# Attention of two pairs of heads as one task on TensorE, with the gates loaded first, more g buffers and a float32 combine

## Chip, cores and metric

The kernel runs on one core of a Trainium2 chip. The metric is the device time of one execution in microseconds. TensorE is called PE in the profile, VectorE DVE, ScalarE ACT, GpSimd POOL; SyncE (SP) issues every DMA of this kernel.

## What is computed

Three layers follow each other, on 4 batches of 576 positions (2304 tokens), 8 heads of 64:

```
scores = q k^T / 8, causal; plus min(-(cum_i - cum_j), 0), cum = cumsum(max(s, 0))
attn   = softmax(scores);  x = attn v            -> 2304 x 512
h      = x w_in;  g = max(h, 0)^2;  x = g w_out  (512 -> 2048 -> 512; int64 views of float64 weights come in)
logits = x phi                                   (32 slots = 8 experts x 4)
slot_input = softmax over tokens(logits)^T x     -> 32 x 512
slot_out[e] = max(slot_input[e] w1[e], 0) w2[e]  (512 -> 1024 -> 512, 8 experts)
out    = softmax over slots(logits) slot_out     -> 2304 x 512
```

## The kernel before

One program does all of it. Every step is a task in a list (`add`) with the buffers that it reads and writes, a cost for each engine that may run it, and a priority. At build time `Plan.run` walks through the list with a clock of its own and writes the engines' instruction order: it takes the task that can start first, among those within `WAIT` the one of lowest priority number, and on TensorE it prefers a task with the tiling that TensorE already has, unless another is `SAME` (6) steps ahead. A task can be placed only when its buffers are free. On the chip each engine runs its list in that order.

The tasks, in the order of the data:

- **Attention.** 80 steps: 4 batches, 5 blocks `i` of 128 queries (the fifth has 64), 4 pairs of heads `p`. `a_scores` (L654 to L700) computes both heads of a pair into two PSUM banks of the pool `ps_s` (four banks); the two heads lie on the two halves of TensorE's rows (tiling 64x128). The maxima are taken on VectorE (L682, L696), `a_exp` (L705) on ScalarE frees the banks, `a_norm` scales, splits into float16 high and low parts (L446) and sends them through a DMA transpose (L746). `a_pv` (L768 to L822) multiplies with V (tiling 128x64, L805) `LAG` (2) steps after the scores. Batch 0 stays in float32 and is transposed on TensorE (L758, through the pool `ps_h`, two banks). Four pairs fill one tile of x.
- **The hidden layer**, for 18 tiles of 128 tokens and 4 column blocks each: `m_h` (L838, 12 matmuls at L847 in two tasks, into a bank of `ps_h`), then relu and square into a buffer `g` (L862 to L866), `m_t` (transposes, L887), `m_l` (logits, L904), and for each two tiles `m_s` (L927: running softmax over tokens, and L966, which reads the eight g buffers of both tiles and frees them). The first evacuation waits for `h_scale` (L828), which needs the scales of all four column blocks of w_in.
- **Weights.** 16 blocks of w_in and 16 of w_out^T are loaded, `N_RAW` (6) ahead, and converted from float64 bits on ACT, POOL and DVE in the first 105 us. When the attention's probability buffers (`p_p`) are done with, their space goes to w_out (16 loads) and to w1 and w2 of the experts (64 pieces of 512 KB, 33.5 MB): more than the space, so later pieces wait until PE has used up something.
- **Experts and combine.** `hidden` (L1277) and `project` (L1295) for each expert; `m_c` (L978) makes the softmax over slots in bfloat16 parts, and `combine` (L1302) multiplies: the slot outputs are split into two bfloat16 parts by DVE (L1312 to L1315), 36 pairs of matmuls (L1326, L1327) write 18 banks, ACT and DVE copy them out, SP sends 12 DMAs.

A partition has 207 KB. By the sizes in the code the pools that are opened at the start take 192,672 bytes; of the 19,296 left `gt` takes five buffers (10,240) and `x` three (6,144), and of what remains one buffer of g (2,048 bytes) fits; the other g buffers come when the pools of the conversion are done with.

Of the kernel before, what the change touches and what calls it, by code (L numbers as in the profile page):

```python
# [7 lines left out]
F32 = mybir.dt.float32  # L8
# [14 lines left out]
N_QK = 2  # L23
D_COST = 1.08
# [9 lines left out]
N_RAW = 6  # L34
SBUF = 207 * 1024
GB1 = 4
GB2 = 8
# [9 lines left out]
N_OB = 5  # L47
# [13 lines left out]
N_W32 = 7  # L61
LAG = 2
# [16 lines left out]
CT_LATE = 0  # L79
# [273 lines left out]
def attention_moe_softmoe(ctx, tc, qk, v, s, w_in, w_out, w_out_t, phi, w1, w2, cst, out):  # L353
# [27 lines left out]
    def fixed(shape, dt):  # L381
# [43 lines left out]
        "vhl": (vhl_p, 5, [128, 2, 512], F16), "ph": (ph_p, 2, [128, 2048], F16), "x2": (x_p, X2, [128, 2, KD, 128], F16), "v": (v_p, 0, [128, 512], F32),  # L425
# [228 lines left out]
    def a_scores(P, i):  # L654


        sel = biases[P]
        if plain(P):
            r, sc, col = raws[P], cs, lambda k: -0.125
            qk = [r]  # L660
            terms = [(lambda d, c: r.t[d, 0, c], lambda d, c: r.t[d, 1, c])]
        else:
            sc, col = scal[P]
            qk = qs, ks = stacks[P]
            terms = [(lambda d, c, e=e: qs.t[d, e, c], lambda d, c, f=f: ks.t[d, f, c]) for e, f in HALVES]
        n = 128 * (i + 1)
        m, nm = small["m"].new(), small["nm"].new()
        pss = [ps_s.new(), ps_s.new()]
        D = [slice(64 * h, 64 * h + 64) for h in range(2)]
        if i < 4:  # L670
            def mul():
                for j, (q_, k_) in enumerate(terms):
                    for h, ps in enumerate(pss):
                        nc.tensor.matmul(ps.t[:, 0:n], q_(D[h], slice(128 * i, 128 * i + 128)), k_(D[h], slice(0, n)), start=j == 0, stop=False)  # L674
                for k in range(2):
                    for h, ps in enumerate(pss):
                        nc.tensor.matmul(ps.t[:, n - 128 + 64 * k:n], rows_h.t[D[h], k, :], mask.t[D[h], k, 64 * k:128], start=False, stop=False)
                for h, ps in enumerate(pss):
                    nc.tensor.matmul(ps.t[:, 0:n], sel.t[D[h], :], cum3.t[D[h], 0:n], start=False, stop=True)  # L679
            add([*qk, sel, mask, cum3, rows_h], pss, P=((5 if plain(P) else 4) * (5 + n / 2.4) + 80, mul), tiling=(64, 128))  # L680
            for h, ps in enumerate(pss):
                add([ps], [(m, 2 + h)], V=(60 + 1.04 * n, lambda ps=ps, h=h: nc.vector.reduce_max(out=m.t[:, 2 + h:3 + h], in_=ps.t[:, 0:n], axis=AX.X)))  # L682
        else:
            for ps, c0, c1 in ((pss[0], 0, 512), (pss[1], 512, 576)):
                def mul(ps=ps, c0=c0, c1=c1):
                    o = [ps.t[d, 0:c1 - c0] for d in D]
                    for j, (q_, k_) in enumerate(terms):
                        for h, d in enumerate(D):
                            nc.tensor.matmul(o[h], q_(d, slice(512, 576)), k_(d, slice(c0, c1)), start=j == 0, stop=False)  # L689
                    if c0:  # L690
                        for h, d in enumerate(D):
                            nc.tensor.matmul(o[h], rows_h.t[d, 0, 0:64], mask.t[d, 0, 0:64], start=False, stop=False)
                    for h, d in enumerate(D):
                        nc.tensor.matmul(o[h], sel.t[d, 0:64], cum3.t[d, c0:c1], start=False, stop=True)
                add([*qk, sel, mask, cum3, rows_h], [ps], P=(880 if c0 == 0 else 180, mul), tiling=(64, 64))
                add([ps], [(m, c0 // 512)], V=(60 + 1.04 * (c1 - c0), lambda ps=ps, c0=c0, c1=c1: nc.vector.reduce_max(out=m.t[:, c0 // 512:c0 // 512 + 1], in_=ps.t[:, 0:c1 - c0], axis=AX.X)))  # L696
            add([(m, 0), (m, 1)], [(m, 2)], V=(65, lambda: nc.vector.tensor_tensor(out=m.t[:, 2:3], in0=m.t[:, 0:1], in1=m.t[:, 1:2], op=ALU.max)))
# [70 lines left out]
    def a_pv(P, i):  # L768
        b, p = P
        if p == 0:  # L770
            xps[b, i] = ps_x0.new()
        x = xps[b, i]
        c0 = 128 * p
        c1 = c0 + (128 if i < 4 else 64)
        mms = []
        if whole(P[0], i):
            vv, pt = [vraw[b, j] for j in range(i + 1)], a_transpose(P, i)
            f = lambda: pt.t.bitcast(F32)
            for j in range(i + 1):
                def two(h, j=j):  # L780
                    k_ = slice(0, 64 if j == 4 else 128)
                    o = 128 * (h * (i + 1) + j) if i < 4 else 128 * j + 64 * h
                    return vv[j].t[k_, 128 * p + 64 * h:128 * p + 64 * h + 64], f()[k_, o:o + c1 - c0]
                mms.append(two)
            ns = 268 * len(mms) - 30 if i < 4 else 170 * len(mms)
        else:
            vv, pt = [vhl[b, j] for j in range(i + 1)], pts.pop((P, i))
            V = lambda e, j, h, k=128: vv[j].t[0:k, e, 128 * p + 64 * h:128 * p + 64 * h + 64]
            T = lambda: pt.t.rearrange("p (j q) -> p j q", q=128)
            for j in range(min(i + 1, 4)):  # L790
                for e, f in ((0, 0), (0, 1), (1, 0)):
                    if i < 4:
                        mms.append(lambda h, j=j, e=e, f=f: (V(e, j, h), T()[:, (2 * h + f) * (i + 1) + j, :]))
                    else:
                        mms.append(lambda h, j=j, e=e, f=f: (V(e, j, h), T()[:, j + 5 * f, 64 * h:64 * h + 64]))
            if i == 4:
                mms.append(lambda h: (V(0, 4, h), T()[:, 4, 64 * h:64 * h + 64]))
                mms.append(lambda h: (V(1, 4, h, 64), T()[0:64, 4, 64 * h:64 * h + 64]))
            ns = (57 if i < 4 else 38) * len(mms) + 10
# [178 lines left out]
    def m_c(t0, n):  # L978

        c1, c4, pc, w = small["c1"].new(), c4_p.new(), ps_t.new("c"), n * NS  # L980
# [4 lines left out]
        part = lambda j: c4.t[:, 0:n, j, :]  # L985
# [8 lines left out]
        for j in range(3):  # L994
            add(L_, [(c4, j)], V=(130 + 0.52 * w, lambda j=j: nc.vector.tensor_copy(out=part(j), in_=c())),
                A=(93 + 0.834 * w, lambda j=j: nc.scalar.copy(out=part(j), in_=c())))
            if j == 0:
                add([(c4, 0)], [(c4, 3)], G=(161 + 0.834 * w, lambda: nc.gpsimd.tensor_copy(out=part(3), in_=part(0))))
            if j < 2:
                add([(c4, j)], L_, V=(60 + 1.04 * w, lambda j=j: nc.vector.tensor_tensor(out=c(), in0=c(), in1=part(j), op=ALU.subtract)))  # L1000
        ph = lambda: pc.t.bitcast(BF16)

        def turn():
            for k in range(n):
                nc.tensor.transpose(ph()[:, k * 128:(k + 1) * 128], c4.t[:, k].rearrange("p a n -> p (a n)"), ident_h.t)
        add([c4, ident_h], [pc], P=(60 * n, turn))
        evacuate(lambda: ct.t[:, t0:t0 + n, :], lambda: ph()[:, 0:n * 128].rearrange("p (t q) -> p t q", q=128), n * 128, [pc], [(ct, t0)], "VA")
# [91 lines left out]
    def prepare(x):  # L1099
# [295 lines left out]
```

## Time and profile before

| | us |
|---|---|
| median of the runs (568.04, 568.16; a third, at 1643.59, stands apart) | 568.16 |
| profiled execution, its time | 565.6 |
| its span, first to last instruction | 563.8 |
| busy in the span: PE / DVE / ACT / POOL | 494.1 / 375.0 / 321.8 / 222.6 |
| moved by DMA | 102.70 MB, mean 182 GB/s |

The profiled execution is one run with the profiler on. "Busy" is the time in which at least one instruction of the engine was in flight; matmuls are pipelined, so a busy PE may still have room. A line number is a line of the kernel before.

### The profile page before, as it was taken

To read this page: it belongs to the slowest core of one execution; us is meant where nothing else is said; L and a number is where in the kernel's file an instruction comes from. 1 tells how busy PE (TensorE), PEld (TensorE's weight loads), DVE (VectorE), ACT (ScalarE), POOL (GpSimd) and SP (SyncE) were. 2 spreads that over 40 slices of the span, in tenths; PEclk is the share of its full clock that TensorE was granted. 3 is DMA by queue.
4 is the path that set the end of the run, shared out by engine and by line. 5 is a ranking of instruction groups with operands and counts; after the bars stand their busy time and mean duration, and the time that the engine had idled before them with its cause. 6 is when DMAs were issued, how large, how long until landed. Compare 5 with 4: busy or idle time off the path is not lost. (4 is left out here: it accounts for less than half of the span.)

```text
span 563.8 us, 13264 instructions
## 1 busy us (share of the span) xinstructions
PE 494.1 (88%) x5025; PEld 277.9 (49%) x5025; DVE 375.0 (67%) x948; ACT 321.8 (57%) x802; POOL 222.6 (39%) x351
## 2 busy tenths in 40 slices
PE   0377688989999999999999999999999989889873
PEld 0244344656555555655546565555554544434333
DVE  2888988979989777899976648986456451210022
ACT  2768777768766675676654555664555545310023
POOL 3478786756425433565662313524132210000000
PEclk9999778999999999999999999999999999989998
DMA  8988566144646753566643113465098999699938
GB/s 254 348 281 293 197 222 195 38 141 128 146 85 123 121 121 71 123 148 136 141 87 74 31 29 57 94 113 94 6 228 306 287 330 382 249 331 409 409 121 335
DMA packets 107464, 102.70 MB, mean 182 GB/s; under 512 B 80904, under 2 KB 81032, under 8 KB 107400
## 3 DMA queue, kind: packets, MB, share of 16 engines
q1 hardware_dynamic: 107400, 101.86, 61.9%
q8 instruction: 39, 0.64, 0.4%
q14 instruction: 25, 0.20, 0.1%
HBM read 77.85 MB, written 4.72 MB: 146 GB/s over the span
## 5 line engine op out<-in xcount | busy, mean ns | idle before, releaser
L847 PE MATMUL bank<-sbuf 128*128 128x512 f16 x864 | 201.7, 379 | 1.3 <-ACT sbuf L820 0.8
L847 PEld LDWEIGHTS <-sbuf 128*128 128x128 f16 x864 | 81.8, 98 | 88.8 <-issue 4.1
L440 POOL TENSOR_SCALAR sbuf<-sbuf 128x512 f16<-128x512 f32 (+9 forms) x128 | 95.6, 753 | 63.4 <-DVE sbuf L728 16.7
L705 ACT ACTIVATE sbuf<-bank,sbuf 128x512 f32<-128x512 f32 (+4 forms) x160 | 93.4, 589 | 40.6 <-DVE sbuf L699 30.6
L457 ACT COPY sbuf<-bank 128x512 f32<-128x512 f32 (+6 forms) x129 | 59.5, 475 | 98.1 <-PE bank L887 31.6
L446 DVE SCALAR_TENSOR_TENSOR sbuf<-sbuf 128x512 f16<-128x512 f32 (+5 forms) x146 | 105.3, 748 | 9.9 <-POOL sbuf L440 9.1
L682 DVE TENSOR_REDUCE sbuf<-bank 128x1 f32<-128x128 f32 (+3 forms) x128 | 57.6, 480 | 5.2 <-PE bank L679 4.9
L674 PE MATMUL bank<-sbuf 64*128 64x128 f16 (+7 forms) x352 | 47.0, 363 | 15.0 <-DMA sbuf<-in_qk_dram 14.1
L727 POOL TENSOR_SCALAR sbuf<-sbuf 128x2 f32<-128x2 f32 (+1 forms) x66 | 18.1, 274 | 106.4 <-ACT sbuf L705 71.5
L862 ACT ACTIVATE sbuf<-bank,sbuf 128x512 f32<-128x512 f32 x56 | 38.4, 686 | 35.2 <-PE bank L847 35.1
L513 POOL TENSOR_SCALAR sbuf<-sbuf 128x512 int32<-128x512 uint8 x47 | 35.6, 757 | 56.5 <-DMA sbuf<-in_w_out_dram 27.5
L805 PE MATMUL bank<-sbuf 128*64 128x128 f16 (+4 forms) x1296 | 55.1, 228 | 1.5 <-DVE sbuf L446 0.7
L458 DVE COPY sbuf<-bank 128x512 f32<-128x512 f32 (+7 forms) x63 | 32.0, 512 | 31.8 <-PE bank L887 18.3
L887 PE MATMUL bank<-sbuf 128*128 128x128 f32 x288 | 45.4, 280 | 5.1 <-POOL sbuf L864 2.0
L463 ACT ACTIVATE sbuf<-sbuf 128x512 bf16<-128x512 f32 (+1 forms) x60 | 39.0, 651 | 13.2 <-DVE sbuf L515 11.5
L515 DVE SCALAR_TENSOR_TENSOR sbuf<-sbuf 128x512 int32<-128x512 int32 x48 | 35.6, 747 | 14.7 <-POOL sbuf L513 11.7
L887 PEld LDWEIGHTS bank<-sbuf 128*128 128x128 f32 x288 | 33.2, 142 | 20.4 <-ACT sbuf L865 3.7
L510 ACT ACTIVATE sbuf<-sbuf 128x512 f32<-128x512 f32 x48 | 31.6, 671 | 16.1 <-DMA sbuf<-in_w_out_dram 7.7
L805 PEld LDWEIGHTS <-sbuf 128*64 128x64 f16 (+1 forms) x1056 | 28.8, 110 | 17.4 <-issue 16.4
L758 PE MATMUL bank<-sbuf 128*128 128x128 f32 (+1 forms) x100 | 19.6, 314 | 14.3 <-POOL sbuf L440 13.1
L705 ACT ACTIVATION_READ_ACCUMULATOR sbuf<-bank,sbuf 128x1 f32 x160 | 32.0, 200 | 0.0
L865 ACT ACTIVATE sbuf<-sbuf 128x512 f32<-128x512 f32 x44 | 27.7, 630 | 4.8 <-DVE sbuf L863 3.7
(140 smaller groups left out, 664.2 us busy)
## 6 DMA issues: line engine op xcount, KB each, us to landing
sbuf<-in_w_dram SPq DMA_DIRECT2D x48, 512.0 KB, 10.1
sbuf<-in_qk_dram SPq DMA_DIRECT2D x16, 576.0 KB, 6.2
sbuf<-in_w_in_dram SPq DMA_DIRECT2D x16, 512.0 KB, 10.1
sbuf<-in_w_out_t_dram SPq DMA_DIRECT2D x16, 512.0 KB, 5.2
sbuf<-in_w_out_dram SPq DMA_DIRECT2D x16, 512.0 KB, 4.4
sbuf<-in_w_dram SPq DMA_DIRECT2D x32, 256.0 KB, 5.4
sbuf<-in_v_dram SPq DMA_DIRECT2D x28, 256.0 KB, 3.0
out_dram<-sbuf SPq DMA_DIRECT2D x8, 512.0 KB, 4.5
```

Source lines behind the costliest of these rows:

```text
L440: "G": (244 + 0.834 * n, lambda: nc.gpsimd.tensor_scalar(out=out_(), in0=in_(), scalar1=scale(), scalar2=1.0, op0=ALU.mult, op1=ALU.mult)),
L446: alts = {"V": (base + 1.04 * n, lambda: nc.vector.scalar_tensor_tensor(out=out_(), in0=in_(), scalar=scale(), in1=hi(), op0=ALU.mult, op1 ...
L457: "A": (51 + 0.834 * n, lambda: nc.scalar.copy(out=out_(), in_=in_())),
L463: add(r + [junk], w, A=(186 + 0.834 * n, lambda: nc.scalar.activation(out=junk.t[:, 0:n], in_=in_(), func=AF.Abs, accum_out=acc_())))
L513: G=(671, lambda: nc.gpsimd.tensor_scalar(out=l.t, in0=low(), scalar1=2.0 ** -5, scalar2=-0.484375, op0=ALU.mult, op1=ALU.add)))
L674: nc.tensor.matmul(ps.t[:, 0:n], q_(D[h], slice(128 * i, 128 * i + 128)), k_(D[h], slice(0, n)), start=j == 0, stop=False)
L682: add([ps], [(m, 2 + h)], V=(60 + 1.04 * n, lambda ps=ps, h=h: nc.vector.reduce_max(out=m.t[:, 2 + h:3 + h], in_=ps.t[:, 0:n], axis=AX.X)))
L705: ex = lambda t, o, n, ps, h, k: add([nm, sc, ps], [t, (sums, k)], A=(373 + 0.834 * n, lambda: nc.scalar.activation(out=t.t[:, o:o + n], i ...
L805: nc.tensor.matmul(x.t[64 * h:64 * h + 64, c0:c1], lhs, rhs, start=n == 0, stop=n == len(mms) - 1)
L847: nc.tensor.matmul(ps.t, X.t[:, e, kd, :], w[c].t[:, kd, :], start=kd == 0 and e == 0 and w is wh, stop=kd == KD - 1 and e == 1)
L862: add([ps, (sc, b)], [g], A=(571, lambda: nc.scalar.activation(out=g.t, in_=ps.t, func=AF.Relu, scale=sc.t[:, b, c:c + 1])), V=(630, lambd ...
L887: nc.tensor.transpose(ps.t[:, j * 128:(j + 1) * 128], g.t[:, j * 128:(j + 1) * 128], ident)
```

## The change

- `a_scores` takes two pairs of heads (`N_S` = 2): one task writes all four banks of `ps_s`, pair after pair, and the maxima follow for both. For the fifth block it is two tasks, each for both pairs. It is called at every second step.
- `a_pv` takes two pairs as well, as one task, and is called one step later (`LAG` 3).
- The loads of the gates s come ahead of the constants and of w_in in the list, the second pair of q and k ahead of the first scores, and pairs three and four at the first step.
- Buffers: g 8 at first and 3 later (4 and 8); raw blocks of the conversion 4 (6), its float32 blocks 6 (7); output buffers 11 (5).
- `m_c` keeps its result in float32 and makes no bfloat16 parts. A new `m_ct` copies the result of up to four pairs of tiles together on POOL, transposes it on TensorE and copies it out. `combine` has no split: four float32 matmuls of 32 rows each (tiling 32x128) work on four tiles into four banks, which come in turn from `ps_s` and from the other pools; with two tiles in one DMA as before.

```diff
-N_RAW = 6
+N_RAW = 4
-GB1 = 4
-GB2 = 8
+GB1 = 8
+GB2 = 3
-N_OB = 5
+N_OB = 11
-N_W32 = 7
-LAG = 2
+N_W32 = 6
+LAG = 3
...
-    def a_scores(P, i):
+    def a_scores(Ps, i):
...
+            work.append((P, sel, sc, col, terms, [ps_s.new(), ps_s.new()], small["m"].new(), small["nm"].new()))
+        every = [ps for w in work for ps in w[5]]
         if i < 4:
             def mul():
+                for P, sel, sc, col, terms, pss, m, nm in work:
+                    for j, (q_, k_) in enumerate(terms):
+                        for h, ps in enumerate(pss):
+                            nc.tensor.matmul(ps.t[:, 0:n], q_(D[h], slice(128 * i, 128 * i + 128)), k_(D[h], slice(0, n)), start=j == 0, stop=False)
...
+            add([*reads, mask, cum3, rows_h], every, P=(len(Ps) * (5 if plain(Ps[0]) else 4) * (5 + n / 2.4) + 80, mul), tiling=(64, 128))
...
         def mul():
-            for n, two in enumerate(mms):
-                for h in range(2):
-                    lhs, rhs = two(h)
-                    nc.tensor.matmul(x.t[64 * h:64 * h + 64, c0:c1], lhs, rhs, start=n == 0, stop=n == len(mms) - 1)
-        add(vv + [pt], [x], P=(ns, mul), tiling=(128, 64))
+            for c0, c1, mms in work:
+                for n, two in enumerate(mms):
+                    for h in range(2):
+                        lhs, rhs = two(h)
+                        nc.tensor.matmul(x.t[64 * h:64 * h + 64, c0:c1], lhs, rhs, start=n == 0, stop=n == len(mms) - 1)
+        add(reads, [x], P=(ns, mul), tiling=(128, 64))
...
+    def m_ct(n, group):
+
+        for k in range(len(group[0])):
+            pc, w, t0 = ps_t.new("c"), 32 * len(group), group[0][k]
+            step = group[1][k] - t0
+            src = lambda t0=t0, step=step: lg.t[:, t0:t0 + step * (len(group) - 1) + 1:step, :]
+            flat = c4_p.new()
+            add([(lg, g[k]) for g in group], [flat], G=(161 + 0.834 * w, lambda src=src, flat=flat, w=w: nc.gpsimd.tensor_copy(out=flat.t[:, 0:len(group)], in_=src())))
+            add([flat, cs], [pc], P=(110, lambda flat=flat, pc=pc, w=w: nc.tensor.transpose(pc.t[0:w, 0:128], flat.t[:, 0:len(group)].rearrange("p j n -> p (j n)"), ident)))
+            evacuate(lambda k=k, n=n, w=w: ct.t[0:w, n, 128 * k:128 * k + 128], lambda pc=pc, w=w: pc.t[0:w, 0:128], 128, [pc], [(ct, n)], "VA")
...
-    next(conv)
-    dma(410, lambda: cs.t, lambda: cst, [], [cs])
     for h in range(2):
         dma(240, lambda h=h: s_sb.t[64 * h:64 * h + 64], lambda h=h: bass.AP(tensor=s.tensor, offset=s.offset + h * S, ap=[[0, 4], [2 * S, B * NP], [1, S]]), [], [(s_sb, h)])
+    dma(410, lambda: cs.t, lambda: cst, [], [cs])
+    next(conv)
     qk_load(pairs[0])
...
+    qk_load(pairs[1])
     bias_select(pairs[0])
-    qk_load(pairs[1])
+    bias_select(pairs[1])
...
-            a_scores(P, i)
+            if x % N_S == 0:
+                a_scores([P_ for P_, _ in steps[x:x + N_S]], i)
...
+            if P3[1] % N_S == N_S - 1:
+                with prio(PR_V):
+                    a_pv([(P3[0], P3[1] - j) for j in range(N_S - 1, -1, -1)], i3)
...
+        for m, group in enumerate(out_groups()):
+            n = len(group[0])
+            obs = [ob_p.new() for _ in group]
             for k in range(n):
+                if (m + k) % 2 == 0:
+                    pos = [ps_s.new("o") for _ in group]
+                else:
+                    pos = [p.new("o") for p in (ps_h, ps_h, ps_x0, ps_t)[:len(group)]]
+                for h in range(2):
+                    def mul(m=m, n=n, k=k, h=h, pos=pos):
+                        for j, po in enumerate(pos):
+                            d, o = slice(32 * j, 32 * j + 32), slice(h * w, h * w + w)
+                            nc.tensor.matmul(po.t[:, o], ct.t[d, m, 0:128 * n].rearrange("p (q k) -> p k q", k=n)[:, k], s4.t[d, o], start=True, stop=True)
+                    add([(ct, m), (s4, h)], [(po, h) for po in pos], P=(1.7 * w + 30, mul), tiling=(32, 128))
+                for po, o_ in zip(pos, obs):
+                    evacuate(lambda k=k, o_=o_: o_.t[:, k, :], lambda po=po: po.t, 512, [po], [(o_, k)])
```

## Rows read from the trace of the kernel before

**Rows 1.** Windows, all engines: busy us (instructions), granted clock, DMA share, GB/s.
```profile
60.00:125.00 65.00, 55.72 (x459) 33.48 (x460) 57.63 (x138) 46.87 (x117) 47.67 (x61) 0.87 0.50 155
125.00:410.00 285.00, 280.98 (x3221) 162.13 (x3220) 226.00 (x592) 181.42 (x465) 121.85 (x195) 1.00 0.48 97
460.00:500.00 40.00, 36.11 (x261) 16.20 (x253) 10.88 (x35) 16.22 (x34) 2.12 (x6) 1.00 0.83 304
```

**Rows 2.** The same view in ten-microsecond windows, before and in the experts' part.
```profile
490.00:500.00 10.00, 7.87 (x65) 2.58 (x64) 3.80 (x16) 2.54 (x9) 0.29 (x1) 1.00 0.57 179
...
520.00:530.00 10.00, 9.89 (x120) 4.03 (x112) 0.75 (x4) 0.37 (x1) 0.94 (x3) 1.00 1.03 408
```

**Rows 3.** Timeline, SP around the attention's end: the first load of w_out.
```profile
408.98 0.57 SPq L433 DMA_DIRECT2D sbuf<-in_w_out_dram  x1
```

**Rows 4.** Timeline, the start: begin, us, instruction, [idle before <- released by].
```profile
2.13 1.36 SPq L433 DMA_DIRECT2D sbuf<-in_s_dram  x2
...
12.07 0.46 DVE L1066 TENSOR_SCALAR sbuf<-sbuf 128x576 f32<-128x576 f32 x1 [4.69 <-DMA sbuf<-in_s_dram]
...
13.29 0.80 PE L674 MATMUL bank<-sbuf 64*128 64x128 f32 x4 [13.29 <-DMA sbuf<-in_qk_dram]
...
18.46 0.29 PE L679 MATMUL bank<-sbuf 64*128 64x128 bf16 x2 [4.21 <-DVE sbuf L1074]
```

**Rows 5.** Windows of line 847 alone (the matmuls of m_h): PE, PEld, clock, DMA.
```profile
45.00:109.00 64.00, 0.00 (x0) 0.00 (x0) 0.87 0.58 192
```

**Rows 6.** Timeline, ACT: the first evacuation of a hidden block.
```profile
66.74 0.69 ACT L862 ACTIVATE sbuf<-bank,sbuf 128x512 f32<-128x512 f32 x1
```

**Rows 7.** Timeline, PE: first and last L805 from 125 to 430, a stretch between.
```profile
130.28 1.99 PE L805 MATMUL bank<-sbuf 128*64 128x64 f32 x40
...
337.68 0.36 PE L805 MATMUL bank<-sbuf 128*64 128x128 f16 x6
337.98 1.47 PE L847 MATMUL bank<-sbuf 128*128 128x512 f16 x6
339.28 0.59 PE L932 MATMUL bank<-sbuf 128*128 128x256 f32 x2
...
341.81 1.46 PE L847 MATMUL bank<-sbuf 128*128 128x512 f16 x6
343.20 0.31 PE L957 MATMUL bank<-sbuf 32*128 32x32 f32 x2
...
421.96 0.75 PE L805 MATMUL bank<-sbuf 128*64 128x64 f16 x28
```

**Rows 8.** Timeline, PE: two steps' scores that stand together already.
```profile
239.17 0.65 PE L674 MATMUL bank<-sbuf 64*128 64x384 f16 x6
239.66 0.25 PE L677 MATMUL bank<-sbuf 64*128 64x128 bf16 x4
```

**Rows 9.** Groups by line (L457 by form): shape, count | busy us, mean ns | idle, releasers.
```profile
L705 ACT ACTIVATE sbuf<-bank,sbuf 128x512 f32<-128x512 f32 (+4 forms) x160 | 93.4, 589 | 40.6 <-DVE sbuf L699 30.6 <-DVE sbuf L728 5.0 <-DVE sbuf L603 1.8
L682 DVE TENSOR_REDUCE sbuf<-bank 128x1 f32<-128x128 f32 (+3 forms) x128 | 57.6, 480 | 5.2 <-PE bank L679 4.9
L705 ACT ACTIVATION_READ_ACCUMULATOR sbuf<-bank,sbuf 128x1 f32 x160 | 32.0, 200 | 0.0
...
L457 ACT COPY sbuf<-bank 128x512 f32<-128x512 f32 x74 | 42.6, 586 | 45.3 <-PE bank L887 31.6 <-PE bank L555 4.0 <-PE bank L758 3.6
```

**Rows 10.** Timeline, the end: combine and first output DMA.
```profile
543.37 0.37 ACT L457 COPY sbuf<-bank 128x256 f32<-128x256 f32 x1 [5.01 <-PE bank L1295]
...
545.23 0.70 PE L1310 MATMUL bank<-sbuf 128*128 128x256 f32 x2 [0.74 <-ACT sbuf L457]
...
547.63 0.27 PE L1327 MATMUL bank<-sbuf 128*128 128x256 bf16 x1 [0.39 <-DVE sbuf L1315]
...
549.04 11.49 SPq L433 DMA_DIRECT2D out_dram<-sbuf  x12
```

**Rows 11.** Windows of one microsecond while the output leaves.
```profile
555.00:556.00 1.00, 0.77 (x7) 0.43 (x5) 0.10 (x2) 0.03 (x2) 0.00 (x0) 1.00 0.94 262
```

More of the change, by code (lines that the diff above doesn't have):

```diff
@@ L23 @@
 N_QK = 2
+N_S = 2
+N_PH = 2
 D_COST = 1.08
@@ L670, in a_scores @@
         if i < 4:
             def mul():
-                for j, (q_, k_) in enumerate(terms):
-                    for h, ps in enumerate(pss):
[L674 to L677, printed above, removed]
@@ L678, in mul @@
-                for h, ps in enumerate(pss):
[L679 to L697, printed above, removed]
@@ L698, in a_scores @@
-        w = 2 if i < 4 else 1
-        add([m, sc], [nm], V=(130, lambda: nc.vector.tensor_scalar(out=nm.t[:, 0:w], in0=m.t[:, 2:2 + w], scalar1=col(5), scalar2=None, op0=ALU.mult)))
-        sm[P, i] = pss, nm
+                for P, sel, sc, col, terms, pss, m, nm in work:
+                    for j, (q_, k_) in enumerate(terms):
+                        for h, ps in enumerate(pss):
+                            nc.tensor.matmul(ps.t[:, 0:n], q_(D[h], slice(128 * i, 128 * i + 128)), k_(D[h], slice(0, n)), start=j == 0, stop=False)
+                    for k in range(2):
+                        for h, ps in enumerate(pss):
+                            nc.tensor.matmul(ps.t[:, n - 128 + 64 * k:n], rows_h.t[D[h], k, :], mask.t[D[h], k, 64 * k:128], start=False, stop=False)
+                    for h, ps in enumerate(pss):
+                        nc.tensor.matmul(ps.t[:, 0:n], sel.t[D[h], :], cum3.t[D[h], 0:n], start=False, stop=True)
@@ new lines, in a_scores, with mul @@
+            add([*reads, mask, cum3, rows_h], every, P=(len(Ps) * (5 if plain(Ps[0]) else 4) * (5 + n / 2.4) + 80, mul), tiling=(64, 128))
+        else:
+            for k, (c0, c1) in enumerate(((0, 512), (512, 576))):
+                def mul(k=k, c0=c0, c1=c1):
+                    for P, sel, sc, col, terms, pss, m, nm in work:
+                        o = [pss[k].t[d, 0:c1 - c0] for d in D]
+                        for j, (q_, k_) in enumerate(terms):
+                            for h, d in enumerate(D):
+                                nc.tensor.matmul(o[h], q_(d, slice(512, 576)), k_(d, slice(c0, c1)), start=j == 0, stop=False)
+                        if c0:
+                            for h, d in enumerate(D):
+                                nc.tensor.matmul(o[h], rows_h.t[d, 0, 0:64], mask.t[d, 0, 0:64], start=False, stop=False)
+                        for h, d in enumerate(D):
+                            nc.tensor.matmul(o[h], sel.t[d, 0:64], cum3.t[d, c0:c1], start=False, stop=True)
+                add([*reads, mask, cum3, rows_h], every if k == 0 else every[1::2], P=(len(Ps) * (880 if c0 == 0 else 180), mul), tiling=(64, 64))
@@ L766, in a_transpose, with a_pv @@
         return pt
-    def a_pv(P, i):
-        b, p = P
-        if p == 0:
+    def a_pv(Ps, i):
+        b, p = Ps[-1]
+        if Ps[0][1] == 0:
             xps[b, i] = ps_x0.new()
[L772 to L799, printed above, removed]
-        def mul():
-            for n, two in enumerate(mms):
-                for h in range(2):
-                    lhs, rhs = two(h)
-                    nc.tensor.matmul(x.t[64 * h:64 * h + 64, c0:c1], lhs, rhs, start=n == 0, stop=n == len(mms) - 1)
-        add(vv + [pt], [x], P=(ns, mul), tiling=(128, 64))
@@ L993, in m_c, with out_groups @@
         add([c1], L_, V=(60 + 1.04 * w, lambda: nc.vector.tensor_tensor(out=c(), in0=c(), in1=wide(), op=ALU.mult)))
[L994 to L1007, printed above, removed]
+    def out_groups():
+        pairs_, ones, t = [], [], 0
+        while t < NTT:
+            if tiles_b[t][0] == tiles_b[t][1]:
+                pairs_.append((t, t + 1))
+                t += 2
+            else:
+                ones.append((t,))
+                t += 1
+        return [pairs_[j:j + 4] for j in range(0, len(pairs_), 4)] + [ones]
+    def m_ct(n, group):
[7 more added lines that the diff above has]
+            evacuate(lambda k=k, n=n, w=w: ct.t[0:w, n, 128 * k:128 * k + 128], lambda pc=pc, w=w: pc.t[0:w, 0:128], 128, [pc], [(ct, n)], "VA")
     h_list = [(t, c) for t in range(NTT - LAST) for c in range(4)] + [(t, c) for c in range(4) for t in range(NTT - LAST, NTT)]
@@ L1211, in w2_load @@
         wt[e, 1] = [u for g in range(4) for u in w_unit(w2[e, 256 * g:256 * g + 256, :].rearrange("(p k) f -> p (k f)", k=2), [])]
-    if not CT_LATE:
-        arena.want(ct_p, 1, [128, NTT, 128], BF16, p_p)
-        arena.want(c4_p, 2, [128, 4, 4, NS], BF16, p_p)
-        for n, (t0, nt) in enumerate(groups):
-            with prio(0 if n < len(groups) - 1 else -100):
-                m_c(t0, nt)
+    arena.want(ct_p, 1, [128, 3, 256], F32, p_p)
+    arena.want(c4_p, 2, [128, 4, NS], F32, p_p)
+    for n, (t0, nt) in enumerate(groups):
+        with prio(0 if n < len(groups) - 1 else -100):
+            m_c(t0, nt)
+    for n, group in enumerate(out_groups()):
+        with prio(-100):
+            m_ct(n, group)
     def tail(n, shape, dt, when):
@@ L1317, in combine @@
-        t = 0
-        while t < NTT:
-            n = 2 if t + 1 < NTT and tiles_b[t] == tiles_b[t + 1] else 1
-            o_ = ob_p.new()
-            for k in range(n):
-                po = ps_s.new()
-                cols = lambda t=t, n=n, k=k: ct.t[:, t:t + n, :].rearrange("p t q -> p (t q)").rearrange("p (q k) -> p k q", k=n)[:, k]
-                for h, o in enumerate(halves):
-                    def mul(cols=cols, o=o, po=po):
-                        nc.tensor.matmul(po.t[:, o], cols()[0:96], sst.t[0:96, 0, o], start=True, stop=False)
-                        nc.tensor.matmul(po.t[:, o], cols(), sst.t[:, 1, o], start=False, stop=True)
-                    add([(ct, (t + j) // 4 * 4) for j in range(n)] + [(sst, h), (sst, 2 + h)], [(po, h)], P=(0.86 * w, mul))
-                evacuate(lambda k=k, o_=o_: o_.t[:, k, :], lambda po=po: po.t, 512, [po], [(o_, k)])
-            b0, b = tiles_b[t]
-            if b0 == b:
-                row = b * S + 128 * sum(q_ == (b, b) for q_ in tiles_b[:t])
-                dma(1500, lambda row=row, n=n: out[row:row + 128 * n, :].rearrange("(p k) d -> p (k d)", k=n), lambda o_=o_: o_.t.rearrange("p k d -> p (k d)"), [o_], [])
-            else:
-                for j, q_ in enumerate((b0, b)):
-                    dma(370, lambda q_=q_: out[q_ * S + S - 64:q_ * S + S, :], lambda j=j, o_=o_: o_.t[64 * j:64 * j + 64, 0, :], [o_], [])
-            t += n
@@ L1342, in attention_moe_softmoe @@
         project(e)
-        if CT_LATE and e == E - 2:
-            for t0, nt in groups:
-                m_c(t0, nt)
     combine()
```

99 lines of the change are left out of this document (65 added, 34 removed).

## The prediction

> **What bounds the kernel now.** I read the page, then windows by stage, then the timeline of each place that the change touches. The reader is to see three regimes. Up to about 125 us PE is not the limit: in 60 to 125 it is busy 55.7 of 65 us, at a granted clock of 0.87 (a mixture of 1.2 and 2.4 GHz), while DVE is busy 57.6 [rows 1]. From 125 to 410 PE is the limit: 281.0 of 285 us at full clock; DVE, the next, has 226.0 [rows 1]. From there on two things run side by side: what is left of the hidden layer on PE, and the stream of w_out, w1 and w2, which may start only when the attention's buffers are done with; SP issues its first load at 408.98 [rows 3]. In 460 to 500 the DMA engines are at 0.83, in the last ten of these at 0.57; from 500 on they are full (1.03, 408 GB/s) until the experts have their weights [rows 1, 2]. So the stream sets the end: 33.5 MB of expert weights don't fit, and before 500 it pauses because PE has not yet freed space. In 460 to 500 it stands still for 0.17 of 40 us, 6.8 us. The end can move in three ways only: the attention ends earlier, PE catches up so that these 6.8 us go, or the piece behind the last weight, 543.37 to 563.8, gets shorter [rows 10].
>
> **The change part by part.** *Gates first.* The loads of s are issued at 2.13, behind 1 MB of w_in, and their first reader starts at 12.07; from there DVE needs 18.46 − 12.07 = 6.4 us until the first scores can end [rows 4]. Those scores wait 4.21 us for it, having waited until 13.29 for q and k. With s ahead, q and k of the first pair, and now of the second too, are next: the scores should end near 14 to 15 in place of 18.5. At most 18.46 − 13.29 = 5.2 us; nothing if s lands no earlier, the time between its issue and its reader being 9.9 us. DVE's chain itself stays. I take −3 us, near the middle, because nothing else is ready in these microseconds.
>
> *More g.* By the code's sizes one g buffer exists until the conversion's pools are done with; two raw blocks less and one float32 block less leave 10,240 bytes more, so six from the start. The trace shows what one costs: not a matmul of the hidden layer between 45 and 109 [rows 5], although its weights and the first tile of x are there (block one ran before 45, and its evacuation was at 66.74 [rows 6]). Half a block is 1.30 us (337.98 to 339.28 [rows 7]), a block 2.6, five blocks 13 us of PE. They would go where PE has 65 − 55.7 = 9.3 us idle and a low clock [rows 1]. Bounds: 0 (ACT and DVE, which must evacuate them, fall behind by as much) and −13. I take −8, near the idle time in the row. The three buffers fewer of the second lot make eleven in place of twelve, and nine are kept after the attention as before: nothing, as two tiles need eight.
>
> *Fewer tasks, fewer changes of tiling.* Half a block takes 1.30 us when the next matmul has the same tiling and 1.39 when it hasn't (341.81 to 343.20): 0.09 us for a change [rows 7]. From 125 to 430 there are 56 runs of L805, the first and the last in [rows 7]; 60 products as 30 tasks leave at most 30, so at least 26 runs go. Of the scores, 39 runs for 60 steps: many steps stand together already, as the pair in [rows 8], so only some six go. A run less saves one change (its neighbours differ) or two (they are the same): 32 runs give 2.9 to 5.8 us, 0 if the order pulls the tasks apart in other ways. I take −4.
>
> *Four banks at once.* New scores need all of `ps_s` and so wait for the last exponential of two steps; before, two steps alternated. For two steps the chain is: the scores, about 1.1 us (two pieces such as 239.17 to 239.66 [rows 8], with mask and bias), two maxima of 0.48 each, four exponentials of 0.59 + 0.20 [rows 9]: 1.1 + 1.0 + 3.2 = 5.3 us without a queue. The stage has 60 steps in 284 us [rows 3, 7], 9.5 us for two. There are 4.2 us for the queues of PE, DVE and ACT; the row's 30.6 us of ACT waiting for DVE over 160 exponentials, 0.8 us for two steps, shows these queues to be short as seen from ACT. I take +2, between 0 and the price of the rival below.
>
> *The rest.* Four raw blocks ahead in place of six: the DMA engines are at 0.50 in 60 to 125 [rows 1], so a block can follow at once; I take +1, bounds 0 and +3, a tenth of a microsecond for each of 32 blocks. The product with V one step later, the float32 blocks of the conversion and the bfloat16 parts of `m_c` that fall away are at nothing: other work of PE fills that wait, and DVE is busy 10.9 of 40 us in 460 to 500 [rows 1]; uncovered, the later product costs one step, 4.7 us, at the end of the attention. `m_ct` adds five POOL copies and transposes behind POOL's 2.1 busy us of that stage.
>
> *Combine.* Before, the second half passes DVE's split, and its last matmul type starts at 547.63, 4.3 us behind the first copy at 543.37; SP issues the first output at 549.04 [rows 10]. Now no half needs the split and its buffer; both copies can go at once on ACT and DVE, and both halves be ready near 545.4. A float32 matmul of 256 columns is about 0.35 us (two in 0.70 [rows 10]); four row tiles of 32 at once make ten such groups, 3.5 us, if they do run together, as the two heads of L674 do: six matmuls of 384 columns in 0.49 us [rows 8], where one after the other, by the 0.22 us of 512 columns (six in 1.30 [rows 7]), they would take 0.98. But four tiles are copied out before the second half of the first DMA: five copies of 0.59 [rows 9] on two engines, three rounds, so the first output leaves at 545.4 + 0.7 + 1.8 = 547.9, 1.1 us earlier. Eleven output buffers take away a dip such as that at 555 (262 GB/s [rows 11]). I take −1; bounds −2 and, with the 36 matmuls one by one (12.6 us, the first tile complete 2.1 us later), +5. The Trainium skill, *TensorE: Matmul & The Clock Gate*, section "Measured speedup vs the span model", has 3.07 and not 4 for four row tiles; the ten groups would then be an estimated 4.6 us in place of 3.5, still less than the output's 11.5 us of issuing. No run here shows four row tiles yet.
>
> **The sum.** PE's hidden layer ends −3 − 8 − 4 + 2 + 1 = −12 us. The attention shares PE with it by priority: of the 12 us freed before 410 it gets about half, so its end moves by −3 − 6 + 2 + 1 = −6. The stream starts 6 earlier; PE, another 6 ahead of that, frees space sooner and gives back 6 of the 6.8 us. Last weight −12, end −13: 565.6 − 13 = 552.6 for the profiled execution, and 568.16 − 13 = 555 for the median, which lies 2.6 above it. About 2% (11.4 us) is what a measurement of this kernel tells from no change.
>
> **Rivals.** (1) *The stream starts no earlier.* Four banks eat what PE gives the attention; only the 6.8 us can be had, half to all of them, and the start's 3 partly: −3 to −7, 561 to 565. For it: the 9.5 us against 5.3 leave less than half for queues of engines that are 64 to 99% busy [rows 1]. The Trainium skill, *TensorEngine Tiling (Array Packing)*, section "PSUM Bottleneck", says that packing speeds up TensorE and not the emptying of its banks; by that rule this is the case that comes, and the rows bear it out only so far as the 3.2 of 5.3 us are ACT's. (2) *Slower: the four banks become the bound.* If queues bring the chain over the pace, 10.5 us for two steps, the 30 double steps of batches 1 to 3 end 30 us later, the stream with them; PE, done sooner, gives back 6.8 and the start 3: +20, 588. It decides from 9.5 + 10/30 = 9.8 us on. Against it: ACT's short waits. (3) *The gain is larger.* If the attention gets all that PE saves, it ends −16 (−3, −13 of the g blocks, −4, +4), the stream keeps its pattern: 565.6 − 17, a median of 545 to 551. For it: PE is 99% busy where the attention runs. (4) *The g buffers do nothing but move a wait.* Two blocks take both banks of `ps_h` from 45 until the scales come at 66.74 [rows 6], the transposes of batch 0 stand behind them, and the 8 are lost again, with 4 to 8 more: 564 to 572.
>
> **How the numbers follow.** Forecast 0.47 (its own range 550 to 561), larger gain 0.17, rival 1 0.18, rival 4 0.07, slower 0.11. The range, 542 to 574, leaves out most of the slower case and the ends. Faster by over 2% (under 556.8) has the larger gain and some seven tenths of the forecast: 0.50; within 2%, 0.38; slower, 0.12.
>
> **What would show it.** L1066 near 6 and L679 before 16; matmuls of L847's successor between 45 and 109, and a clock above 0.87 in 60 to 125; at most 30 runs of the products from 125 to 430; the first load of w_out at about 403; the DMA share near 1 in the 40 us ahead of the experts; the first output 5 us after the last expert matmul. I am wrong if PE shows waits for exponentials ahead of the scores, if w_out starts after 409, or if the last stage lengthens because the four row tiles don't overlap.

## Result and the profile after

The changed kernel takes 555.67 us (median of 4 runs, 554.79 to 555.86) against 569.3 for the kernel before on the same chip (median of all four runs): a ratio of 0.9765, 95% interval 0.9733 to 0.9796. One run of the kernel before, at 1643.59, and one of the experiment f_e_g, at 734.88, stand far apart and are left out of the ratios. The changed kernel is faster by 2.0 to 2.7%. The profiled execution took 555.68 us, its span 553.9 us against 563.8.

Windows of the changed kernel, in the stretches of [rows 1, 2] (columns as there):

```profile
60.00:125.00 65.00, 56.38 (x471) 33.82 (x469) 59.58 (x141) 44.95 (x114) 47.76 (x59) 1.00 0.53 168
125.00:410.00 285.00, 278.08 (x3298) 164.13 (x3298) 239.27 (x611) 175.24 (x459) 126.43 (x205) 1.00 0.50 102
460.00:500.00 40.00, 35.50 (x337) 17.06 (x338) 5.06 (x17) 13.73 (x31) 0.78 (x3) 1.00 0.97 362
```

PE is as busy as before from 60 to 125 us, but at full clock (1.00 for 0.87), and the DMA engines hardly pause from 460 to 500 (0.97 for 0.83). Timeline of the changed kernel: the start, the last two exponentials of batch 1, the first load of w_out and the end (answers to [rows 3, 4, 10]).

```profile
1.20 1.36 SPq L434 DMA_DIRECT2D sbuf<-in_s_dram  x2
...
9.17 0.46 DVE L1085 TENSOR_SCALAR sbuf<-sbuf 128x576 f32<-128x576 f32 x1 [5.90 <-DMA sbuf<-in_s_dram]
...
15.73 0.29 PE L680 MATMUL bank<-sbuf 64*128 64x128 bf16 x2 [1.84 <-DVE sbuf L1093]
...
215.76 0.78 ACT L711 ACTIVATE sbuf<-bank,sbuf 128x512 f32<-128x512 f32 x1
...
216.52 0.41 ACT L711 ACTIVATE sbuf<-bank,sbuf 128x64 f32<-128x64 f32 x1
...
399.32 0.59 SPq L434 DMA_DIRECT2D sbuf<-in_w_out_dram  x1
...
534.71 0.37 ACT L458 COPY sbuf<-bank 128x256 f32<-128x256 f32 x1 [5.46 <-PE bank L1313]
535.11 0.42 DVE L459 COPY sbuf<-bank 128x256 f32<-128x256 f32 x1 [4.80 <-ACT sbuf L458]
535.13 1.16 PE L1327 MATMUL bank<-sbuf 128*128 128x256 f32 x4 [0.47 <-ACT sbuf L458]
536.29 5.50 PE L1341 MATMUL bank<-sbuf 32*128 32x256 f32 x72
539.08 11.91 SPq L434 DMA_DIRECT2D out_dram<-sbuf  x12
```

L680 ends the first scores 2.7 us earlier than L679 did. Nothing of that is left at the end of batch 1: its last exponential is at 216.52, in the kernel before at 206.84 (ACT's timeline):

```profile
206.84 0.41 ACT L705 ACTIVATE sbuf<-bank,sbuf 128x64 f32<-128x64 f32 x1
```

Yet SP issues the first load of w_out 9.7 us earlier (399.32 for 408.98), the last expert matmul gives way to the combine 8.7 us earlier (534.71 for 543.37), and the first output leaves 4.4 us behind that in place of 5.7. The hidden layer's matmuls alone (windows restricted to L858; answer to [rows 5], then from 0):

```profile
45.00:109.00 64.00, 14.33 (x55) 5.57 (x56) 0.91 0.58 189
0.00:125.00 125.00, 18.60 (x72) 7.12 (x72) 0.95 0.67 219
```

A block is 12 of these matmuls, so 6 blocks stand ahead of 125 us; before, there were 29 records, 2.4 blocks:

```profile
0.00:125.00 125.00, 6.90 (x29) 2.69 (x30) 0.93 0.67 220
```

### The profile page after: what moved, and what is told of

Same layout as the page of the kernel before. It is cut to its first block, busy times and chain, and to the rows that moved or that the text cites. A ratio compares the mean times of both kernels' runs of the same rounds, so it can differ in the third digit from the quotient of the medians.

```text
span 553.9 us, 13197 instructions
## 1 busy us (share of the span) xinstructions
PE 480.1 (87%) x5012; PEld 272.0 (49%) x5012; DVE 376.8 (68%) x939; ACT 305.2 (55%) x774; POOL 226.3 (41%) x356
## 4 chain that ended last, share of the span: by engine, by line
PE 36%; DVE 5%; DMA 5%; ACT 2%; issue 2%; POOL 1%; DVEq 0%; ACTq 0%; POOLq 0%; SPq 0%
PE bank L858 17%; DMA sbuf<-in_w_dram 4%; PE bank L898 3%; PE bank L816 3%; PE bank L1295 2%; PE bank L915 2%; PE bank L675 2%; PE bank L1313 1%; PE bank L977 1%; DVE sbuf L447 1%; DMA sbuf<-in_w_out_dram 1%; DVE sbuf L459 1%; ACT sbuf L458 1%; PE bank L689 1%; PE bank L1274 1%
## 5 line engine op out<-in xcount | busy, mean ns | idle before, releaser
L858 PE MATMUL bank<-sbuf 128*128 128x512 f16 x864 | 204.6, 381 | 0.8 <-ACT sbuf L458 0.7
L858 PEld LDWEIGHTS <-sbuf 128*128 128x128 f16 x864 | 81.6, 98 | 88.2 <-issue 8.5
L441 POOL TENSOR_SCALAR sbuf<-sbuf 128x512 f16<-128x512 f32 (+8 forms) x131 | 96.9, 746 | 65.8 <-DVE sbuf L734 24.2
L458 ACT COPY sbuf<-bank 128x512 f32<-128x512 f32 (+5 forms) x129 | 58.3, 465 | 105.0 <-PE bank L898 28.3
L733 POOL TENSOR_SCALAR sbuf<-sbuf 128x2 f32<-128x2 f32 (+1 forms) x68 | 20.8, 305 | 100.1 <-ACT sbuf L711 72.8
L675 PE MATMUL bank<-sbuf 64*128 64x128 f16 (+7 forms) x352 | 43.5, 344 | 15.5 <-DMA sbuf<-in_qk_dram 13.6
L816 PE MATMUL bank<-sbuf 128*64 128x128 f16 (+4 forms) x1296 | 48.7, 225 | 1.4 <-DVE sbuf L459 1.4
L873 ACT ACTIVATE sbuf<-bank,sbuf 128x512 f32<-128x512 f32 x47 | 32.2, 685 | 29.7 <-PE bank L858 29.4
L459 DVE COPY sbuf<-bank 128x512 f32<-128x512 f32 (+3 forms) x65 | 31.7, 505 | 24.0 <-PE bank L898 10.9
L511 ACT ACTIVATE sbuf<-sbuf 128x512 f32<-128x512 f32 x48 | 31.5, 675 | 20.3 <-DMA sbuf<-in_w_in_dram 9.7
L764 PE MATMUL bank<-sbuf 128*128 128x128 f32 (+1 forms) x100 | 19.2, 310 | 22.3 <-POOL sbuf L441 17.4
L816 PEld LDWEIGHTS <-sbuf 128*64 128x64 f16 (+1 forms) x1056 | 27.9, 110 | 10.9 <-issue 9.8
L1304 DVE TENSOR_SCALAR sbuf<-bank 128x32 f32<-128x32 f32 x8 | 1.5, 190 | 39.2 <-PE bank L1301 38.9
```

The source lines that it names most:

```text
L441: "G": (244 + 0.834 * n, lambda: nc.gpsimd.tensor_scalar(out=out_(), in0=in_(), scalar1=scale(), scalar2=1.0, op0=ALU.mult, op1=ALU.mult)),
L458: "A": (51 + 0.834 * n, lambda: nc.scalar.copy(out=out_(), in_=in_())),
L459: "V": (68 + 1.04 * n, lambda: nc.vector.tensor_copy(out=out_(), in_=in_())),
L858: nc.tensor.matmul(ps.t, X.t[:, e, kd, :], w[c].t[:, kd, :], start=kd == 0 and e == 0 and w is wh, stop=kd == KD - 1 and e == 1)
```

## Experiments

Twelve kernels, in four groups that each ran on one chip; every ratio is against the kernel before on the same chip. The kernel before is hardly the same twice (563.7 to 573.0 us over these runs); the changed one keeps within 553.4 to 556.8.

**e_g**, old buffers in the changed kernel:

```diff
-N_RAW, N_W32, GB1, GB2 = 4, 6, 8, 3
+N_RAW, N_W32, GB1, GB2 = 6, 7, 4, 8
```

> The changed kernel with the old buffers alone: six raw blocks, seven float32 blocks, four g buffers (one at the start), eight later. Theory 1 (the g buffers bring most of it: 3.6 blocks more of the hidden layer are done at 125 us in the changed kernel, at 2.6 us each, 9.4 us): the time goes back by 6 to 9, to 562 to 565 us, with no matmul of m_h between 45 and 109 us. Theory 2 (the pairs bring most, by 37 changes of tiling fewer from 125 to 430 us): 556 to 558 us.

Measured: 563.77 us, ratio 0.9934 (0.9904 to 0.9964). As theory 1 has it; two blocks stand ahead of 125 us, one of them in the stretch from 45 to 109 where the theory had none.

**e_ns1**, one pair at a time in the changed kernel:

```diff
-N_S, LAG = 2, 3
+N_S, LAG = 1, 2
```

> The changed kernel with scores and products again one pair at a time, the product two steps behind; gates, buffers and combine as changed. Theory 1: the pairs bring nothing, since the attention fell about 10 us behind in the middle of the changed kernel (exponential 81 at 216.5 against 206.8 us before): 551 to 557 us, with exponential 81 back near 205 us. Theory 2: the changes of tiling come back (about 179 runs from 125 to 430 us): 560 to 564 us.

Measured: 567.71 us, 0.9989 (0.9956 to 1.0022). Both theories fall short: without the pairs all is gone, the g buffers' part too, although 4.5 blocks stand ahead of 125 us and the last exponential of batch 1 (the expectation's 81) is back at 208.3.

**b_gs**, gates first and new buffers in the kernel before:

```diff
+load s, then cst, then the first block of w_in
-load the first block of w_in, then cst, then s
-N_RAW, N_W32, GB1, GB2 = 6, 7, 4, 8
+N_RAW, N_W32, GB1, GB2 = 4, 6, 8, 3
```

> The kernel before with two parts alone: gates first, and the new buffers (raw 4, float32 6, g 8 and 3). Theory 1: 558 to 561 us, near all of the gain but the end of the combine (1 us). Theory 2: 565 to 568 us, a gain at the start that is lost later.

Measured: 567.91 us, 1.0015 (0.9985 to 1.0044). Theory 1 is wrong here and theory 2 has the time: the buffers and the gates together bring nothing. They do what they should (the first exponential is 2.7 us earlier, 4.5 blocks ahead of 125 us), but batch 0 ends at 133.4 in place of 125.7.

**ctl**, a planner's priority:

```diff
-PR_W = 60
+PR_W = 62
```

> The changed kernel with one priority of the planner that concerns only the last weights changed from 60 to 62. Both theories: 555.7 us within 1. If it moves by more, the order alone is worth that much, and smaller differences of the other runs tell nothing.

Measured: 554.41 us, 0.9779 (0.9741 to 0.9816). The edit left the order of every engine's instructions as it was, so this is the changed kernel a second time and says nothing of other orders.

**f_e_g, f_b_gs, f_after**: extra matmuls, one into each bank, ahead of the scores of batch 0, in e_g, b_gs and the changed kernel.

```diff
+        if Ps[0][0] == 0 and i < 4:
+            def fill():
+                for ps in every:
+                    nc.tensor.matmul(ps.t, ident_h.t, cum3.t[:, 0:512], start=True, stop=True)
+            add([ident_h, cum3], every, P=(215 * len(every), fill))
```

> The changed kernel with the old buffers (as e_g) and, ahead of the scores of the first four query blocks of batch 0, one matmul of 512 columns into each bank that the scores then overwrite: 32 matmuls, some 7 us of PE's work, where PE is not the limit. Theory 1 (clock: in e_g PE was busy for 33.9 us at 1.2 GHz ahead of the last m_h and in the changed kernel for 11.2, so 17 against 5.6 us lost, which is the 11 to 13 us between them): with PE fed, the stretches at half clock between 45 and 130 us go, and the time falls from 563.8 to 555 to 559 us. Theory 2 (the blocks of m_h done early are the gain by themselves, and the clock only follows): 562 to 567 us, whatever the clock shows.

> The kernel before with gates first, the new buffers (as b_gs) and the same extra matmuls. Theory 1: b_gs lost 8.6 us to the low clock, 5 of them in batch 0, and has 74 runs of equal tiling more than the changed kernel (6.6 us): 562 to 565 us. Theory 2: 566 to 571 us.

> The changed kernel with the same extra matmuls. Theory 1: it lost 5.6 us to the low clock, near 5 of them from 42.6 to 56.3 us: 551 to 555 us. Theory 2: 555 to 560 us, the extra work added.

Measured: 581.27 us, 1.0229 (1.0147 to 1.0311); 570.14, 1.0026 (0.9986 to 1.0066); 573.92, 1.0108 (1.004 to 1.0176). The 32 matmuls were not 7 us of work: they took 12.7 (f_b_gs), 13.9 (f_after) and 13.9 us (f_e_g) of PE, as 14, 24 and 26 of them ran at 1.2 GHz, wholly or in part. In f_b_gs (theory 2's time) they cost nothing that can be measured: b_gs has 1.0015, and batch 0 ends at 132.9 for 133.4. So in that kernel and order PE did have room in batch 0. With the pairs neither theory had the time: f_e_g and f_after are some 17 and 18 us slower than e_g and the changed kernel, and the last exponential of batch 0 is at 138.6 in place of 126.1 and at 139.9 in place of 125.8. What is put ahead of the scores of two pairs there, ahead of all four banks, delays the whole attention. The order differs too, so the 18 us are not the work alone. Nor does the clock explain the times: PE's busy time at 1.2 GHz up to the hidden layer's last matmul grew only in the changed kernel (25.3 to 48.0 us); it fell from 51.5 to 45.8 in e_g, which still lost 17 us, and from 34.4 to 30.0 in b_gs. (These sums count the start of the execution, which the expectations leave out; see the account of PE.)

**e_s1**, scores by one pair, products by two:

```diff
-N_S = 2
+N_S, N_PV = 1, 2   # a_pv asks for N_PV
```

> The changed kernel with scores again one pair at a time and the products of two pairs as one task. Theory A (changes of tiling: the products carry most of what the pairs save, some 26 of 37 runs): 556 to 559 us. Theory B (scores on four banks cost time, seen in the attention's lag of 10 us in batch 1): 550 to 555 us, exponential 81 near 207 us in place of 216.5.

Measured: 566.07 us, 0.9978 (0.9939 to 1.0018). Neither: the products stand in 32 runs of one tiling as in the changed kernel, and that alone brings nothing either.

By now every kernel but the changed one stood near the kernel before, so its order as such came under suspicion. **a_wait, b_wait**: the planner's constant, in the changed kernel and in the kernel before; **a_lat**: a third order of the changed kernel; **e_g_wait**: a second order of e_g.

```diff
-WAIT = 100
+WAIT = 110          # a_wait, b_wait, e_g_wait
-    "P": {"P": 3, "V": 197, "A": 197, "G": 197, "D": 197},
+    "P": {"P": 3, "V": 200, "A": 197, "G": 197, "D": 197},   # a_lat
```

> The changed kernel with one constant of the planner's choice among ready tasks changed from 100 to 110 ns: the same tasks, buffers and engines' work in another order (from PE's 94th instruction on). Theory 3 (a good part of the 13 us is this one order: every kernel with another order that was run, five of them, came to 564 to 574 us, with 8.6 to 21 us lost to the low clock against 5.6): 559 to 566 us, with 8 us or more lost to the low clock. Theory 1b (the parts of the change bring it, so that an order as such is worth 2 us): 553 to 558 us.

> The kernel before with the same constant changed from 100 to 110 ns, another order of the same tasks. Theory 3: the kernel before stands on a good order as well, so this one is slower: 570 to 576 us. Theory 1b: 565 to 569 us.

> The changed kernel in a third order: the planner takes 200 in place of 197 ns from the end of a matmul to its reader on DVE. Theory 3b (the change is worth some 8 us in any order, and one order against another up to 5): 555 to 562 us. Theory 3 (the 13 us were this one order): 563 to 567 us. In either case the first load of w_out sets the end: last w load some 121 to 128 us behind it.

> The changed kernel with the old buffers (as e_g) and the planner's constant 110 in place of 100, so e_g in another order. Theory 3b (the g buffers are worth some 4 us in any order with pairs): 560 to 566 us, that is 2 to 8 us over the changed kernel with the same constant (560.3), with 2 blocks of m_h at 125 us in place of 5.9. Rival (the g buffers bring nothing, e_g was a bad order): 555 to 560 us.

Measured: a_wait 560.29 us, 0.9864 (0.9813 to 0.9916); b_wait 570.32, 1.0027 (0.9994 to 1.006); a_lat 560.07, 0.9863 (0.9808 to 0.9917); e_g_wait 569.94, 1.0024 (0.9985 to 1.0062). So both are true in part; e_g_wait is slower than either of its ranges. With all its parts the kernel gains 1.4% (about 8 us) in two other orders; the remaining 5 us belong to the one order that it came with. The g buffers, pairs given, are worth 9 us in two orders (0.9934 against 0.9779 on one chip; 1.0024 against 0.9864 with the other constant, each against its own runs of before). Without pairs they are worth nothing (b_gs, e_ns1), and pairs without them nothing to 4 us. The kernels without one half or the other (b_gs, e_ns1, e_s1) ran in one order each, and an order can be worth 5 us.

**An account of PE** puts this together. Up to the first load of w_out, taken from PE's instructions and the record of the granted clock in each profiled execution: the time in which PE did nothing; half of its busy time at 1.2 GHz; and 0.09 us for each stretch of equal tiling, the price in [rows 7]. (In the kernel before, from 130 to 420 us, a matmul of L847 is followed after 216 ns by one of its own tiling and after 309 to 312 ns by one of any other.)

The record of the clock begins with the first rise to full clock, at 35 to 56 us, and the windows count the time ahead of it as 1.00. It is not: a_lat's record begins at 56.05, and six matmuls of L858 take 2.72 us ahead of that, as in the changed kernel at 52.88, where the record says 0.50, and 1.46 behind it (PE's timeline of a_lat):

```profile
52.55 2.72 PE L858 MATMUL bank<-sbuf 128*128 128x512 f16 x6
...
59.32 1.46 PE L858 MATMUL bank<-sbuf 128*128 128x512 f16 x6
```

So the time ahead of the record counts as 1.2 GHz here.

```
kernel     parts        first w_out  idle  low clock  tilings          sum
before     none         409.0        45.5  15.8       244 x 0.09 22.0  83.3
b_wait     none         406.8        45.8  13.5       259        23.3  82.6
b_gs       gates, g     407.8        45.3  15.5       259        23.3  84.1
e_ns1      gates, g     403.7        44.4  18.7       259        23.3  86.4
e_s1       g, products  404.3        46.4  17.8       216        19.4  83.6
e_g        pairs        407.8        48.0  21.2       200        18.0  87.2
e_g_wait   pairs        416.7        50.6  21.3       194        17.5  89.4
after      all          399.3        48.4  10.9       194        17.5  76.8
ctl        all          399.9        46.4  14.2       194        17.5  78.1
a_wait     all          406.3        41.5  13.5       198        17.8  72.8
a_lat      all          403.2        48.9  13.9       193        17.4  80.2
```

All parts together lose 73 to 80 us, every other kernel 83 to 89. The pairs of both kinds take away some 5 us of changing tilings; without the g buffers these come back, most of them as low clock (21 us for 11 to 14). Without the pairs the g buffers leave the low clock where it was (15.5 for 15.8) or higher. Each row is one execution: after and ctl have the same order and differ by 3.3 us in low clock, and e_g's is the slowest of its ten. Nor is the sum the kernel's time, as more or less work is done by then. (a_wait spent its gain differently: it had 57.5 blocks done at 406.3 where the others had 52 to 56, and its stream started late.) The windows of 40 to 130 us show it, first e_g and then e_g_wait (clock 0.83 and 0.85 with the time ahead of the record, 43.2 us in both, at half):

```profile
40.00:130.00 90.00, 70.23 (x562) 45.76 (x562) 78.10 (x182) 61.31 (x162) 70.66 (x85) 0.85 0.52 168
```

```profile
40.00:130.00 90.00, 69.45 (x522) 43.58 (x520) 77.03 (x172) 61.90 (x157) 63.83 (x83) 0.87 0.48 162
```

and then the changed kernel and a_lat (0.92, and 0.89 in place of the 0.98 that the window says):

```profile
40.00:130.00 90.00, 72.03 (x612) 43.55 (x609) 80.59 (x187) 63.85 (x168) 68.05 (x86) 0.92 0.56 180
```

```profile
40.00:130.00 90.00, 69.94 (x541) 42.04 (x538) 79.00 (x171) 60.87 (x156) 67.40 (x85) 0.98 0.55 175
```

What it looks like is plain in PE's timeline, first of e_g:

```profile
62.15 0.41 PE L764 MATMUL bank<-sbuf 128*128 128x128 f32 x2 [2.28 <-ACT sbuf L458]
63.61 0.64 PE L764 MATMUL bank<-sbuf 128*128 128x128 f32 x2 [1.05 <-ACT sbuf L873]
64.18 1.65 PE L675 MATMUL bank<-sbuf 64*128 64x384 f32 x4
...
71.52 0.90 PE L764 MATMUL bank<-sbuf 128*128 128x128 f32 x3 [2.73 <-POOL sbuf L441]
72.22 1.92 PE L478 MATMUL bank<-sbuf 128*128 128x128 f32 x8
```

and of the changed kernel:

```profile
61.30 1.06 PE L478 MATMUL bank<-sbuf 128*128 128x128 f32 x8
64.11 0.63 PE L764 MATMUL bank<-sbuf 128*128 128x128 f32 x4 [1.76 <-ACT sbuf L873]
65.17 1.46 PE L858 MATMUL bank<-sbuf 128*128 128x512 f16 x6 [0.42 <-ACT sbuf L458]
...
71.29 0.92 PE L675 MATMUL bank<-sbuf 64*128 64x384 f32 x4
```

In e_g PE waits 2.28 and 2.73 us for the transposes' input, and the same four score matmuls take 1.65 us, the eight of L478 1.92; in the changed kernel half blocks of the hidden layer stand between the waits, and they take 0.92 and 1.06. That the blocks *keep* the clock up is the reading of these rows, not shown by itself: the extra matmuls, meant to show it, came ahead of the scores and not into the gaps, and b_gs, e_ns1 and e_s1, with 4.5 blocks done ahead of 125 us, have no less low clock than the kernel before. How the pairs and the g buffers work together stays open; that both are needed is what the times show.

## Why the prediction came true, and where it did not

The time was right, 555.67 for 555, and the medians differ by 12.5 us (555.67 from the 568.16 of the forecast) for 13. The profiled span was not as right: forecast −13 us from 565.6, measured −9.9. The profiled execution before lay 2.6 us under its median, while the one after lies on it, so that offset belongs to one execution and the traces below explain 9.9 us. Part of the hit is luck: in two other orders (a_wait, a_lat) the same parts gain 8 us and not 13, and the terms of the sum did not come as forecast.

**Gates first**, −3: L680 came 2.7 us earlier than L679, and L1085 at 9.17, not near 6. But the term should not have been added to the end: the last exponential of batch 0 is where it was, at 125.8 for 125.7, also in e_g (126.1). The gates were not tried by themselves.

**More g**, −8: the blocks came as forecast (55 matmuls from 45 to 109, clock 1.00 from 60 on), and the size agrees with the 9 us measured with pairs. The step that failed is the one that sized it: the blocks "would go where PE has 65 − 55.7 = 9.3 us idle and a low clock". Idle time to the first load of w_out didn't fall (45.5 to 48.4 us). The low clock did (15.8 to 10.9), and only beside the pairs. Without them (b_gs, e_ns1) the term measured nothing.

**Fewer changes of tiling**, −4: near its size. From 125 to 430 us the products stand in 32 runs for 56 (at most 30 were expected), all tilings in 171 for 198, which at 0.09 us is 2.4; up to w_out 50 stretches fewer make 4.5 us. That it could be had without the g buffers was wrong.

**Four banks**, +2: as a wait it isn't there. What PE waited for from 125 to 410 in the changed kernel (in total, times, longest):

```profile
PE bank L968 <- ACT sbuf L958: 2.2, 2, 1.4
PE bank L816 <- DVE sbuf L459: 1.4, 1, 1.4
...
PE bank L943 <- ACT sbuf L711: 0.6, 1, 0.6
```

The scores' lines L675 to L694 do not appear. The attention does fall 10 us behind in batch 1, and e_ns1 without pairs does not (208.3); but e_s1, with scores by single pairs, is at 213.6, so the banks are not all of it. How much of it is theirs stays open. The rival built on them (588 us) fell. By the rule of the Trainium skill, *TensorEngine Tiling (Array Packing)*, "PSUM Bottleneck", the emptying of the banks may become the bottleneck; these rows show no such wait.

**Stream.** The hidden layer's last matmul was to move by −12 and moved from 484.5 to 475.7, −8.8. The attention's end (−6) moved by −7, its last exponential from 410.5 to 403.5, and the first load of w_out by −9.7. From there the forecast splits the gain wrongly: 6 of 6.8 idle us were to be given back. Between first load of w_out and last weight issue lie 123.1 us before and 123.7 after: the pauses from 460 to 500 went, others ahead of them came. The trace of a_wait shows the stream's start as a limit: its hidden layer ended at 472.3, the earliest of all, but its stream began at 406.26, and its last weight was issued at 527.4 against 523.0:

```profile
406.26 0.58 SPq L434 DMA_DIRECT2D sbuf<-in_w_out_dram  x1
```

This start-to-last distance was 121 to 131 us in all kernels, so the start sets the end only to within some 10 us. It is not the only limit. In e_ns1 the stream starts 5.3 us earlier than in the kernel before, and its last weight is issued 2.7 us later (534.8 for 532.1):

```profile
403.65 0.57 SPq L435 DMA_DIRECT2D sbuf<-in_w_out_dram  x1
...
515.14 20.00 SPq L435 DMA_DIRECT2D sbuf<-in_w_dram  x16
```

Its hidden layer ended 4.6 us later (489.5 for 484.9). From the end of the hidden layer's last matmul to the last weight issue lie 47.2 us before, 46.9 after, and 45 to 49 in all kernels but a_wait (54.7) and f_e_g (56.8), whose distances from the start, 121.1 and 121.6, are among the shortest. Read over these fourteen traces, the end is set by whichever comes later: the hidden layer's end and some 47 us, or the stream's start and some 121. So the forecast's path, that PE done sooner frees space sooner, fits these traces, with 8.8 us for 12.

**Combine**, −1: the first output came 4.4 us after the last expert matmul for 5.7, −1.3. The four row tiles do run together (the first nine groups of four start mostly 0.22 us apart), but their term was too small: 5.50 us for 36 matmuls, not 3.5 (each of these float32 matmuls is two records, so x72; I had read L1310's two as two). One after the other, a record of 128 float32 columns takes 0.11 us (L764 in the timelines above: four in 0.63, two in 0.41); 72 of 256 columns would take an estimated 15.8, so the gain is about 2.9 over the whole stretch; its later groups start 0.26 to 0.46 apart. The Trainium skill, *TensorE: Matmul & The Clock Gate*, "Measured speedup vs the span model", states 3.07 for four row tiles of 512 columns; the estimate of 2.9 lies near it. It cost nothing, as the output's issuing takes 11.91 us.

**Rivals.** Rival 1 (no earlier start) and 3 (545 to 551) didn't come. Rival 4 fell for the changed kernel; e_ns1 and b_gs are much like it, blocks done early without any gain. What I didn't foresee is that an order by itself is worth 5 us, more than any term of the sum but that of the g buffers.

## What to carry to other kernels

Two parts that each remove something can be worth nothing or little alone and 8 us together (here perhaps because one brings the work that fills the gaps which the other leaves): try them together before dropping one. Count an engine's lost time by kind (idle, low clock, changes) up to the event that releases the next stage; whether a busy share of 86% with the clock at 0.87 leaves room, the share doesn't say: the same extra matmuls cost 18 us in one kernel and nothing in another. Look at where the record of the clock begins before reading a granted clock of 1.00. With a planned order, run each version in two or three orders before crediting a difference of under 1% to an edit.

## What was not expected of the hardware

Ahead of the first rise the record of the granted clock is empty and the windows read 1.00, while PE runs at 1.2 GHz (half blocks of 2.72 us in a_lat for 1.46 later). Thirty-two extra matmuls in batch 0 went with 18 us more in the changed kernel and with nothing in b_gs. A float32 matmul shows as two records in the trace; 36 of 256 columns on four row tiles took 5.50 us, against the estimated 15.8 above.
